# Six jobs instead of five in the lead-in of an attention-plus-FFN kernel, and a new token order for its last two units

## The chip, the cores and the metric

The kernel runs on one core of a Trainium2 chip. The metric is the device time of one execution in microseconds. Three executions of the kernel before took 1590.14, 1590.25 and 1590.91 us; the median is 1590.25 us.

## The reference

`x` has 2048 rows of 512 floats. Two branches read it, and a gate mixes them:

```python
g = sigmoid((x * gate_w).sum(-1, keepdims=True))
# A: 32 query heads of 16, one shared key head and one shared value head
q = (x @ wq).reshape(B, S, 32, 16).transpose(0, 2, 1, 3)
k, v = x @ wk, x @ wv
p = softmax(einsum("bhqd,bkd->bhqk", q, k) * 16 ** -0.5)
a = einsum("bhqk,bkd->bhqd", p, v).transpose(0, 2, 1, 3).reshape(B, S, 512) @ wo
# B: bilinear FFN, 512 -> 1792 -> 512
b = ((x @ w_gate) * (x @ w_up)) @ w_down
out = g * a + (1 - g) * b
```

## The kernel before

**Units.** The attention is cut into 64 units. A unit is one block of 128 query rows for eight heads, which sit in four slots of two. It has 16 steps. For each step two small row-tiled matmuls of the *first pass* (`p1`, L759, then a row maximum on VectorE, L760) and two of the *second pass* (`p2`, L800, then an exponential on ScalarE, L801) are made. One uses the upper half of the array's rows and one the lower half: the kernel calls the halves *lanes* 0 and 1. Matmuls on different lanes run beside each other; matmuls on one lane follow each other. Every two steps, one *token* `p` (`pv`, L813) multiplies the exponentials by V. After a unit's last maximum, four short VectorE instructions (`p1_end`, L765 to L789) and two small DMAs put the row maxima into the unit's query tile, and only then can its second pass begin.

**Jobs.** Everything else that TensorE does is cut into *jobs*: query projections (12 products), FFN gate and up projections (12), down projections (9 or 12) and output projections (12). Each product is done in two halves of 64 rows, one on each lane, into one PSUM bank: first all products of the job on one lane, later all on the other. When both lanes are through, the bank is copied out (`finish`, `evac`). `ffn_jobs` (L606) yields the jobs in a fixed order, so the number of lane slots in the whole program is given; it is only chosen where they stand.

**Front (L826 to L878).** Transposes, the key and value projections and the first two query projections run on the whole array. Between them stand three bursts of maxima, made by `steps(banks)` with 4, 6 and 4 matmuls on the banks that it is given. Together these are 7 of the 16 steps of unit 0.

**Lead-in (the loop at L1063).** Before any second-pass matmul, the first pass must be ahead: `LEAD` is 25 steps per lane. While VectorE works through those maxima, `lead_job` (L1028) and `lead_fill` (L1038, its matmul is L1052) fill TensorE with jobs. At most `OPEN` = 2 jobs may be begun and not ended, and `FIRST` = 5 jobs are begun altogether. A job's second lane may start only when the program can be sure that the first has ended (`E.known`). The last job begun gets one lane only; its other lane is left to the units, so that lane 1 runs one job behind lane 0 from there on. The loop ends when the 25 steps, the five jobs and all second lanes but the last are done. Two transposes of V (`v_late`, L313) also fall into it.

**Units (L1081).** From then on the program follows strings of tokens, one string per unit. `a` and `b` issue a maximum on lane 0 and 1, `c` and `d` a second-pass matmul, `e` and `f` a job's product (L962), `p` the P by V product. Each of the 62 strings `ORDER`, `ORDER_NINE` and `ORDER_AFTER` has 16 each of a, b, c and d, 36 each of e and f, and 8 p. `ORDER_LAST` covers the last two units: 7 a, 7 b, 32 c, 32 d, 72 e, 84 f and 16 p. The tail (L1097) ends the last output projection.

**Queues.** Each engine works its instructions off in the order in which the program emits them: a TensorE instruction that waits for a bank holds back everything behind it. `claim` (L467) picks the bank by a model of when banks come free; on the chip the wait is for the instruction that last read the bank.

Of the kernel before, what the change touches and what calls it, by code (L numbers as in the profile page):

```python
# [31 lines left out]
LEAD = 25  # L32
# [11 lines left out]
PV_IN, PV_ROUND, PV_LAST, PV_END, PV_OUT = 325.0, 866.0, 438.0, 617.0, 647.0  # L44
NB = 8
LAT, LAT_LAST = 1.0, 0.5
FIRST = 5
OPEN = 2


ORDER = (
# [9 lines left out]
    "fcffeeffecffafefcebcfebcfafefdefafccfebfeadeffebcbapppdcbadcppbcbadapppb"  # L61
)
ORDER_LAST = (
    "cdebefebefefedededebbcfefefebefedaefefefadcfefafcfefafefedadefebefedefcf"
    "efcfafabefefedcffefcfefedccfeffcfedefcpppppdedcfefcfcfefefefedefeedcfefe"
    "dfedcpppefedededeffefefededefedefefedcfcffcfefededdefefcfcffedfcfefefefe"
    "fcfpppfcfcffcdfdfcfcdfffccfcfppppp"
)
HALVES = (slice(0, 64), slice(64, 128))
COLS = (slice(0, 256), slice(256, 512))  # L70
# [5 lines left out]
def mix_kernel(ctx: ExitStack, tc: tile.TileContext, x, wq, wk, wv, wo, wg, wu, wd, gw, out):  # L76
# [78 lines left out]
    def mm_all(p, prods, start=True, stop=True):  # L155
        for i, (l, r) in enumerate(prods):
            nc.tensor.matmul(p, l, r, start=start and i == 0, stop=stop and i == len(prods) - 1)  # L157
# [6 lines left out]
    def bank(i, name):  # L164
        return psum.tile([128, 512], F32, name=name, tag=f"bank{i}")
# [130 lines left out]
    def kv(c, b):  # L296
        p = ms_bank(b)
        prods = proj((wkvh, wkvl), xT[c])
        if c == 0:
            prods = prods[0::3] + prods[1::3] + prods[2::3]  # L300
        mm_all(p, prods)
        Kc = KK[:, c * 512:(c + 1) * 512]
        kvs[c] = w512("gs", F32, 3)
        nc.scalar.activation(Kc, p, AF.Identity, bias=kneg)
        nc.scalar.copy(kvs[c], p)
        if c < 2:
            nc.vector.scalar_tensor_tensor(Kc, Kc.bitcast(F32), klow, kvs[c], op0=OP.mult, op1=OP.add)
        else:
            scr = w512("hf", F32, 1)
            nc.gpsimd.tensor_scalar(scr, Kc.bitcast(F32), klow, None, op0=OP.mult)  # L310
            nc.gpsimd.tensor_tensor(Kc, scr, kvs[c], op=OP.add)
# [12 lines left out]
    def v_trans(c, b):  # L324
        pv = bank(b, "pv")
        for t in range(4):
            nc.tensor.transpose(pv[:, t * 128:(t + 1) * 128], kvs[c][:, t * 128:(t + 1) * 128], ident)  # L327
        (nc.vector.tensor_copy if c == 0 else nc.scalar.copy)(
            V[:, c * 4:(c + 1) * 4, 0:DH].rearrange("p t (h d) -> p t h d", h=2),
            pv.rearrange("p (t h c) -> p t h c", t=4, h=2)[:, :, :, 50:58])  # L330
# [88 lines left out]
    def peek():  # L419
        if st["next"] is None and st["gen"] is not None:  # L420
            st["next"] = next(st["gen"], None)
            if st["next"] is None:
                st["gen"] = None
        if front and ready(front[0]) and (len(front) > 1 + (st["f"] > 9) and not st["tail"] or not ready(st["next"])):
            return front[0]
        return st["next"] if ready(st["next"]) else None
# [323 lines left out]
    def p1(k, half, b):  # L750
        u, slot, kq = order1[k]
        c, g, t = units[u]
        q = Q[u]
        if u not in mx:
            mx[u] = work.tile([128, 8, 4], F32, name="mx", bufs=2)
            left[u] = 32
        p = bank(b, "s1")
        r = KROWS[half]
        nc.tensor.matmul(p, q[r, slot], KK[r, kq * 512:(kq + 1) * 512], start=True, stop=True)  # L759
        nc.vector.tensor_reduce(mx[u][:, half * 4 + slot, kq:kq + 1], p, axis=AX.X, op=OP.max)  # L760
        left[u] -= 1
        if left[u] == 0:
            p1_end(u)

    def p1_end(u):  # L765
        q = Q[u]
        m = mm[u % 2]
        nc.vector.tensor_reduce(m[:, 0:8], mx.pop(u), axis=AX.X, op=OP.max)
        w = work.tile([128, 3, 32], F32R, name="mt", bufs=2)
        mt = w[:, 0].bitcast(F32)  # L770
        nc.vector.transpose(mt, m)
        nc.vector.tensor_reduce(w[:, 1], mt.rearrange("p (q v) -> p q v", v=1), axis=AX.X, op=OP.max, negate=True)
        with nc.allow_low_precision(reason="the low part of two that are kept"):
            nc.vector.tensor_reduce(w[:, 2], w[:, 0:2].bitcast(F32).rearrange("p v q -> p q v"), axis=AX.X, op=OP.add)
        end = spend("dve", 800.0)
        d = dram.tile([2, 8, 128], F32, name="dm", tag="dm", bufs=2)

        def store():
            for b in range(4):
                nc.sync.dma_start(d[:, :, b * 32:b * 32 + 32].rearrange("v c q -> c v q"),  # L780
                                  w[b * 32:b * 32 + 8, 1:3].bitcast(F32))
            later(3200, fetch)

        def fetch():
            for half in range(2):
                r = half * 64 + 48
                nc.sync.dma_start(q[r:r + 2].bitcast(F32), d[:, half * 4:half * 4 + 4, :])
            mat[u] = clock["T"] + 4000.0
        later(end - clock["T"] + 300.0, store)  # L789
# [63 lines left out]
    done = 0  # L853

    def steps(banks):
        nonlocal done
        for i, b in enumerate(banks):
            p1(done + i // 2, i % 2, b)
        done += len(banks) // 2

    p = ms_bank(0)
    prods = proj(wqs[1], xT[0])
    mm_all(p, prods[:4], True, False)
    steps((3, 7, 1, 6))
    mm_all(p, prods[4:], False, True)
    qs, qh, ql = w512("wdn", F32, 2), w512("oh", F32R, 2), w512("ol", F32R, 2)
    nc.scalar.copy(qs, p)
# [4 lines left out]
    kv(2, 4)  # L872
    sums.append(gate_mul("wn", 4))
    v_trans(1, 2)
    steps((3, 7, 1, 6))
    kv(3, 0)
    for f in sums:
        f()  # L878
# [11 lines left out]
    qat.update({0: 0.0, 1: 5000.0})  # L890
    st["gen"] = ffn_jobs()
    E = State()
    E.n1, E.dve, E.act = [done, done], 100.0, 3000.0
    E.free = [1700.0, 0.0, 0.0, 0.0, 0.0, 0.0, 200.0, 0.0]
    fetched = 2

# [129 lines left out]
    began, cur = [], [None, None]  # L1026

    def lead_job(l):  # L1028
        if cur[l]:
            return cur[l]  # L1030
        for j in began[:FIRST - 1]:
            if j.first != l and j.done[l] == 0 and j.end is not None and j.end <= E.known:
                return j
        if len(began) < FIRST - l and sum(j.done[1 - j.first] < len(j.items) for j in began) < OPEN and peek():
            return took
# [24 lines left out]

    run, pos, hole, late = [], [0, 0], [0], [0]
    took = object()
    while min(E.n1) < LEAD or len(began) < FIRST or any(cur) or any(j.done[1 - j.first] == 0 for j in began[:-1]):  # L1063
        l = 0 if E.nl[0] <= E.nl[1] else 1
        k = E.n1[l]
        some = (k < LEAD and k <= E.n1[1 - l] + (k >= NJ) and (k < NJ or min(E.n1) >= NJ)
                and max(qat.get(order1[k][0], 1e18), kat[order1[k][2]]) <= clock["T"])
        job = lead_job(l)
        if some and (E.dve < E.nl[l] + 1300.0 or not job) and min(E.free) < E.nl[l]:
            token("ab"[l])  # L1070
        elif job:
            events_until(min(E.nl))
            lead_fill(l)
        else:
            E.nl[l] += 30.0
            events_until(min(E.nl))
    st["lead"] = None
    run += [(began[-1], i) for i in range(len(began[-1].items))]
    pos[0] = len(run)
    is_nine = False  # L1080
    while E.npv < NS:  # L1081
# [15 lines left out]
    while events or front or st["gen"] or st["next"]:  # L1097
        run_events()
        if peek():
            j = take()  # L1100
# [28 lines left out]
```

## Time and profile before

| | us |
|---|---|
| median of three executions | 1590.25 |
| the profiled execution | 1590.37 |
| its span, first to last instruction | 1588.6 |
| TensorE busy | 1582.9 |
| VectorE busy | 1363.4 |
| ScalarE busy | 1203.7 |
| GpSimd busy | 733.3 |

The profiled execution took 1.8 us more than its span, which lies before the first and behind the last instruction. In the rows, PE is TensorE's matmuls, PEld its weight loads, DVE VectorE, ACT ScalarE, POOL GpSimd, SP the engine that issues DMAs; an L with a number is a line of the kernel. Matmuls on different lanes overlap, and each is shown with its whole way through the array, so that a busy PE row says little of how many matmuls were issued in a stretch; it is the starts that count.

### The profile page before, as it was taken

How to read it: one execution, taken by the hardware profiler on the slowest of the kernel's cores; microseconds unless marked ns; L12 is line 12 of the kernel's file. 1: busy time of each engine (PE TensorE's matmuls, PEld its weight loads, DVE VectorE, ACT ScalarE, POOL GpSimd, SP SyncE). 2: the span in 40 equal slices, each digit the busy share in tenths (PEclk: the TensorE clock that was granted, in tenths of full speed). 3: DMA queues.
4: the chain of work that ended last, by engine and by line, in shares of the span. 5: the costliest groups of instructions: out<-in, count | busy, mean ns of one | idle time of the engine just before them, and what ended most of it. 6: DMA issues, size and time to landing. Idle time of an engine off the chain costs nothing.

```text
span 1588.6 us, 35467 instructions
## 1 busy us (share of the span) xinstructions
PE 1582.9 (100%) x13144; PEld 1034.0 (65%) x13144; DVE 1363.4 (86%) x2412; ACT 1203.7 (76%) x2384; POOL 733.3 (46%) x871
## 2 busy tenths in 40 slices
PE   9999999999999999999999999999999999999999
PEld 7775666665665666676675666676675666676675
DVE  6998898898898898898898898888898898888982
ACT  5787787787787787787787787777787787787775
POOL 7535737353633624454532725454442615555440
PEclk9999999999999999999999999999999999999999
DMA  6553322122232212121232212122132212212111
GB/s 196 190 174 119 93 62 74 40 71 58 67 103 79 73 56 67 53 76 54 60 103 72 74 55 73 48 70 66 54 117 65 74 55 74 61 57 59 36 31 42
DMA packets 184995, 121.21 MB, mean 76 GB/s; under 512 B 46197, under 2 KB 154613, under 8 KB 184822
## 3 DMA queue, kind: packets, MB, share of 16 engines
q1 hardware_dynamic: 183620, 118.61, 25.0%
q8 instruction: 104, 1.70, 0.4%
q14 instruction: 69, 0.57, 0.1%
q10 hardware_dynamic: 1202, 0.33, 0.1%
HBM read 82.70 MB, written 36.17 MB: 75 GB/s over the span
## 4 chain that ended last, share of the span: by engine, by line
PE 99%; DVE 1%; DMA 0%; issue 0%; DVEq 0%
PE ms L962 33%; PE acc L813 29%; PE s L800 17%; PE s L759 17%; PE ms L157 1%; PE ms L1052 1%; DVE mx L760 0%; PE px L285 0%; DMA P<-in_A_x_dram 0%; DMA kvn<-in_A_wk_dram 0%; PE wo L157 0%; PE pv L327 0%; PE pick L726 0%; DVE y L737 0%; DVEq L1125 0%
## 5 line engine op out<-in xcount | busy, mean ns | idle before, releaser
L760 DVE TENSOR_REDUCE mx<-s 128x1 f32<-128x512 f32 x2048 | 1289.1, 685 | 172.7 <-PE s L759 94.1
L801 ACT ACTIVATE P<-s 128x512 f32<-128x512 f32 x2048 | 1058.5, 626 | 260.6 <-PE s L800 210.8
L800 PE MATMUL s<-Q,KK 50*128 50x512 f32 x2048 | 703.7, 407 | 0.0
L759 PE MATMUL s<-KK,Q 48*128 48x512 f32 x2048 | 698.4, 401 | 0.2
L813 PE MATMUL acc<-P,V 128*32 128x512 f32 x4096 | 480.5, 597 | 0.0
L800 PEld LDWEIGHTS s<-Q,KK 50*128 50x128 f32 x2048 | 355.8, 185 | 118.4 <-ACT P L801 40.8
L759 PEld LDWEIGHTS s<-KK,Q 48*128 48x128 f32 x2048 | 351.3, 185 | 107.0 <-issue 52.0
L962 PE MATMUL ms<-xh,wl 64*128 64x512 f32 x896 | 319.2, 392 | 0.0
L962 PE MATMUL ms<-xh,wh 64*128 64x512 f32 x896 | 314.2, 393 | 0.0
L962 PE MATMUL ms<-xl,wh 64*128 64x512 f32 x896 | 303.9, 391 | 0.0
L813 PEld LDWEIGHTS acc<-P,V 128*32 128x32 f32 x4096 | 116.8, 109 | 254.8 <-issue 222.8
L397 POOL TENSOR_TENSOR y<-y,yt 128x512 f32<-128x512 f32 x58 | 74.8, 1289 | 212.8 <-ACT yt L396 198.3
L962 PEld LDWEIGHTS ms<-xh,wh 64*128 64x128 f32 x896 | 160.2, 185 | 12.7 <-issue 0.8
L583 POOL TENSOR_TENSOR hf<-gs 128x512 f32<-128x512 f32 x56 | 72.3, 1291 | 203.1 <-ACT gs L572 203.1
L962 PEld LDWEIGHTS ms<-xh,wl 64*128 64x128 f32 x896 | 159.0, 186 | 7.4
L680 POOL TENSOR_TENSOR oT<-raw,rb 128x128 f32<-128x128 f32 x63 | 29.1, 461 | 291.7 <-DMA rb<-dr 285.6
L962 PE MATMUL ms<-wdh,hl 64*128 64x512 f32 x448 | 158.4, 393 | 0.0
L962 PEld LDWEIGHTS ms<-xl,wh 64*128 64x128 f32 x896 | 151.1, 186 | 9.5
L962 PE MATMUL ms<-wdl,hh 64*128 64x512 f32 x448 | 155.3, 394 | 0.0
L962 PE MATMUL ms<-wdh,hh 64*128 64x512 f32 x448 | 155.1, 393 | 0.0
L145 POOL TENSOR_TENSOR wl<-wn,wh 128x512 fp32r<-128x512 f32 x116 | 149.5, 1289 | 9.3
L821 ACT COPY osb<-acc 128x512 f32<-128x512 f32 x63 | 37.0, 588 | 91.5 <-PE acc L813 87.7
(181 smaller groups left out, 1369.3 us busy)
## 6 DMA issues: line engine op xcount, KB each, us to landing
do<-osb SPq DMA_DIRECT2D x63, 256.0 KB
wn<-in_B_w_gate_dram SPq DMA_DIRECT2D x56, 256.0 KB
wn<-in_B_w_up_dram SPq DMA_DIRECT2D x56, 256.0 KB
wdn<-in_B_w_down_dram SPq DMA_DIRECT2D x56, 256.0 KB
Q<-dq SPq DMA_DIRECT2D x384, 32.0 KB
raw<-do SPq DMA_DIRECT2D x252, 32.0 KB
dq<-oh SPq DMA_DIRECT2D x16, 256.0 KB
dq<-ol SPq DMA_DIRECT2D x16, 256.0 KB
```

Of the source, the lines that this page charges most:

```text
L145: nc.gpsimd.tensor_tensor(lo, src, hi.bitcast(F32), op=OP.subtract)
L157: nc.tensor.matmul(p, l, r, start=start and i == 0, stop=stop and i == len(prods) - 1)
L397: nc.gpsimd.tensor_tensor(y[c, t], y[c, t], tmp, op=OP.add)
L583: nc.gpsimd.tensor_tensor(hf, gu[0], gu[1], op=OP.mult)
L680: nc.gpsimd.tensor_tensor(dst, raw[:, 0], rb, op=OP.mult)
L759: nc.tensor.matmul(p, q[r, slot], KK[r, kq * 512:(kq + 1) * 512], start=True, stop=True)
L760: nc.vector.tensor_reduce(mx[u][:, half * 4 + slot, kq:kq + 1], p, axis=AX.X, op=OP.max)
L800: nc.tensor.matmul(p, KK[r, j * 128:(j + 1) * 128], q[r].rearrange("p s q -> p (s q)"), start=True, stop=True)
L801: nc.scalar.activation(P[s][:, half], p, AF.Exp, scale=0.25)
L813: nc.tensor.matmul(acc[u][b:b + 32, :], V[:, j + i], src[:, half], start=(j == 0), stop=(j == NJ - 2))
L821: nc.scalar.copy(osb, acc.pop(u))
L962: nc.tensor.matmul(j.p, lhs[HALVES[l]], rhs[HALVES[l]], start=(l == 0 and i == 0), stop=(l == 1 and end))
```

## The change

Three parts. (1) The bursts of maxima in the front are 5, 6 and 5 matmuls long in place of 4, 6 and 4; the added one stands on bank 5 both times; `steps` now counts matmuls and not steps. (2) In the lead-in, six jobs are begun in place of five, and three may be open at a time in place of two; the condition of the loop now lets the last but one job too be left with lane 1 not begun, and whatever is left so goes to the units. (3) `ORDER_LAST` is a new string with 7 a, 7 b, 32 c, 32 d, 60 e, 72 f and 16 p. The blocks of p in it are 2, 6, 3 and 5 long; they were 5, 3, 3 and 5.

```diff
-FIRST = 5
-OPEN = 2
+FIRST = 6
+OPEN = 3
...
 ORDER_LAST = (
-    "cdebefebefefedededebbcfefefebefedaefefefadcfefafcfefafefedadefebefedefcf"
-    "efcfafabefefedcffefcfefedccfeffcfedefcpppppdedcfefcfcfefefefedefeedcfefe"
-    "dfedcpppefedededeffefefededefedefefedcfcffcfefededdefefcfcffedfcfefefefe"
-    "fcfpppfcfcffcdfdfcfcdfffccfcfppppp"
+    "adefefecfbafefedcbebedefeefedafedefcfefededebafefefefcfafedefebcdefebfae"
+    "fcfedefafebefcfefcfcfeffefcdefedcfcdefcfppcdcdcdppppppfcdeffeededefedffe"
+    "fedefedefedcfefddedcfefefefcfedefeffededefcfefcfcfcpppfcdcfffcfcdffcfcfc"
+    "fdfcfppppp"
 )
...
     def steps(banks):
         nonlocal done
-        for i, b in enumerate(banks):
-            p1(done + i // 2, i % 2, b)
-        done += len(banks) // 2
+        for b in banks:
+            p1(done // 2, done % 2, b)
+            done += 1
...
-    steps((3, 7, 1, 6))
+    steps((3, 7, 1, 6, 5))
...
-    steps((3, 7, 1, 6))
+    steps((3, 7, 1, 6, 5))
...
-    E.n1, E.dve, E.act = [done, done], 100.0, 3000.0
+    E.n1, E.dve, E.act = [done // 2, done // 2], 100.0, 3000.0
...
-    while min(E.n1) < LEAD or len(began) < FIRST or any(cur) or any(j.done[1 - j.first] == 0 for j in began[:-1]):
+    while min(E.n1) < LEAD or len(began) < FIRST or any(cur) or any(j.done[1 - j.first] == 0 for j in began[:-2]) or began[-2].first and not began[-2].done[0]:
...
-    run += [(began[-1], i) for i in range(len(began[-1].items))]
+    run += [(j, i) for j in began if j.done[1] == 0 for i in range(len(j.items))]
```

## Rows read from the trace of the kernel before

**Rows 1.** The page: engines with busy us, share and instructions; shares of the chain.

```profile
PE 1582.9 (100%) x13144; PEld 1034.0 (65%) x13144; DVE 1363.4 (86%) x2412; ACT 1203.7 (76%) x2384; POOL 733.3 (46%) x871
...
PE 99%; DVE 1%; DMA 0%; issue 0%; DVEq 0%
```

**Rows 2.** The chain that ended last, 20 to 75 us: start, us, what.

```profile
39.23 1.17 PE pv L327 x8
...
40.89 6.07 DVE mx L760 x10
...
49.74 0.49 PE s L759
```

**Rows 3.** Busy time by stretch: stretch, its length, busy us (instructions) of each engine.

```profile
35.24:56.61 21.37, 21.12 (x153) 16.37 (x153) 20.47 (x37) 13.44 (x34) 18.92 (x16) 1.00 0.33 120
56.61:72.52 15.91, 15.91 (x130) 13.10 (x131) 15.34 (x28) 14.32 (x29) 5.26 (x6) 1.00 0.74 270
...
81.58:96.28 14.70, 14.70 (x128) 13.14 (x132) 14.23 (x25) 14.43 (x29) 4.54 (x7) 1.00 0.75 250
```

**Rows 4.** Line 1052: duration min/median/max in ns, first and last start.

```profile
L1052 PE MATMUL ms<-hh,wh x20: 383/388/396, 44.2 to 55.9; 64*128 64x512 f32 x20
...
L1052 PE MATMUL ms<-xh,wh x16: 386/394/500, 35.2 to 43.5; 64*128 64x512 f32 x16
```

**Rows 5.** Timeline, one lane's products in a row: start, us, engine, line, what.

```profile
54.00 0.39 PE L1052 MATMUL ms<-hh,wh 64*128 64x512 f32 x1
...
54.23 0.39 PE L1052 MATMUL ms<-hh,wl 64*128 64x512 f32 x1
```

**Rows 6.** Busy time by stretch: two stretches of the lead-in.

```profile
47.65:50.08 2.43, 2.19 (x11) 1.08 (x9) 2.41 (x5) 0.80 (x4) 2.43 (x3) 1.00 0.32 111
...
54.70:56.61 1.91, 1.90 (x11) 1.22 (x10) 1.91 (x4) 1.20 (x3) 1.34 (x2) 1.00 0.26 73
```

**Rows 7.** Timeline of VectorE in and behind the lead-in (idle before, and its releaser).

```profile
36.01 10.94 DVE L760 TENSOR_REDUCE mx<-s 128x1 f32<-128x512 f32 x18 [1.35 <-PE s L759]
...
46.98 0.19 DVE L768 TENSOR_REDUCE mm<-mx 128x8 f32<-128x32 f32 x1
...
51.40 20.39 DVE L760 TENSOR_REDUCE mx<-s 128x1 f32<-128x512 f32 x32
```

**Rows 8.** Timeline of the front around the first and second burst, and one later GpSimd row.

```profile
24.88 0.18 PEld L759 LDWEIGHTS s<-KK,Q 48*128 48x128 f32 x1 [0.18 <-DVE wol L150]
25.14 0.67 ACT L289 COPY osb<-px 128x512 f32<-128x512 f32 x1
...
25.30 0.19 PEld L157 LDWEIGHTS ms<-xh,wl 128*128 128x128 f32 x1 [0.25 <-issue]
...
27.88 3.68 DVE L760 TENSOR_REDUCE mx<-s 128x1 f32<-128x512 f32 x6 [0.63 <-PE s L759]
...
33.75 1.29 POOL L311 TENSOR_TENSOR KK<-hf,gs 128x512 fp32r<-128x512 f32 x1
```

**Rows 9.** Busy time by stretch: the last two units and the tail.

```profile
1536.33:1549.61 13.28, 13.28 (x116) 12.47 (x119) 10.64 (x20) 12.12 (x24) 5.07 (x6) 1.00 0.10 32
1549.61:1554.04 4.43, 4.43 (x43) 1.20 (x42) 0.86 (x2) 1.77 (x4) 0.00 (x0) 1.00 0.05 8
1554.04:1558.21 4.17, 4.17 (x39) 3.31 (x42) 0.00 (x0) 3.64 (x8) 0.46 (x1) 1.00 0.05 16
1558.21:1560.92 2.71, 2.71 (x27) 0.68 (x26) 0.00 (x0) 1.85 (x4) 0.00 (x0) 1.00 0.00 0
1560.92:1569.48 8.56, 8.56 (x72) 7.27 (x75) 1.70 (x3) 8.39 (x17) 0.20 (x1) 1.00 0.33 109
...
1572.19:1575.86 3.67, 3.67 (x28) 2.73 (x31) 0.92 (x2) 3.21 (x7) 0.47 (x1) 1.00 0.06 18
...
1580.29:1588.59 8.30, 4.61 (x57) 3.86 (x56) 3.04 (x7) 0.37 (x1) 0.00 (x0) 0.90 0.10 34
```

**Rows 10.** Timeline of ScalarE across the first block of p there.

```profile
1546.86 4.51 ACT L801 ACTIVATE P<-s 128x512 f32<-128x512 f32 x9
```

## The prediction

> **What bounds the kernel now.** I read the page first: TensorE is busy for nearly the whole span and carries 99% of the chain of work that ended last [rows 1]. A busy TensorE says little here, since two lanes overlap, so I next priced a lane. Where one lane runs alone, its products start 0.23 us apart [rows 5]; the time of a stretch is then the slots of the fuller lane times 0.231 us, plus what is lost. For an ordinary unit this closes: up to its first block of p the string has 62 tokens on lane 0, 62 x 0.231 = 14.3 us, and the stretch took 14.70 us [rows 3]. So the 62 ordinary units are bound by lane slots, and their slots don't change. What can change is the two ends, and there I read the chain in order of time, then stretches, then VectorE's timeline.
>
> The lead-in, 35.24 to 56.61 us, is the one place where the chain leaves TensorE: 6.07 us of it run over ten maxima, and TensorE goes on at 49.74 us after maxima again [rows 2]. VectorE has no idle time there: 18 maxima in 10.94 us (0.60 us each, back to back), then the short instructions that close unit 0 from 46.98 us, then maxima again [rows 7]. TensorE is not full: 47.65 to 50.08 us holds 11 matmuls and 54.70 to 56.61 us another 11, where 21 and 16 had room on two lanes [rows 6]. The reader should see that the first of these is a shortage of jobs, not of time: with two jobs open and neither second lane released, the program could emit only maxima, and those waited for VectorE.
>
> By lanes: line 1052 issued 3 x 20 + 3 x 16 = 108 products (one row of each kind stands in [rows 4]); 60 of them are lane 0's (five jobs of 12). With 18 of the 36 maxima, lane 0 has 78 slots, 18.0 us; the late transposes take 1.2 us [rows 2]; 21.4 - 18.0 - 1.2 leaves 2.2 us lost. The first unit's stretch before its first p, 56.61 to 72.52 us, took 15.91 us against 14.70 us in the next unit [rows 3]: 1.2 us more, because VectorE was still behind. So 3.4 us are lost up to 72.52 us; that is all the room there is for a sixth job.
>
> **Part 1, the bursts.** Each added maximum makes an odd burst, one more slot on the whole-array path: 2 x 0.23 us. But the first burst's fifth stands on bank 5, whose last reader is the ScalarE copy of the last transposed block. That copy runs from 25.14 to 25.81 us, while the burst's fourth matmul loads weights at 24.88 us and the projection behind it resumes at 25.30 us [rows 8]. TensorE works in order, so the fifth waits until about 25.86 us and the eight projection products queue behind it: they resume 0.42 us after the last weight load, as now, so at about 26.28 us, 0.98 us later. That holds the added slot of the first burst too. Bounds: 0.23 us if the copy were out of the way, 1.0 us if it isn't; I take 0.98, since the copy's end is a row. The second odd slot adds 0.23, as bank 5 is then free before its turn. VectorE's idle 0.63 us before the second burst [rows 8] hides the fifth maximum. The key block that the lead-in's first maximum now needs (step 8) is done at 35.04 us [rows 8], later by the same 1 us, and the lead-in begins at 36.45 us: no wait, margin 0.4 us. Sum: lead-in 1.2 us later, two maxima fewer in it. For VectorE that is nothing: 2 x 0.60 = 1.2 us saved, 1.2 us lost at the start.
>
> **Part 2, the lead-in.** Lane 0 now has six jobs of 12 and 17 maxima: 89 slots, 20.6 us, plus 1.2 us of transposes. With a third job open, the starved stretch fills; I take 0.5 us lost in place of 2.2 (bounds 0.2 and 1.5: never none, since the pauses around the transposes and the last job's single lane stay, and not above most of today's). That is 22.3 us from 36.45 us: the lead-in ends at 58.75 us, 2.1 us later. VectorE's 34 maxima and the closing of unit 0 end at about 37.2 + 20.4 + 0.9 = 58.5 us, so it is no longer behind, and the first unit should take 14.8 us in place of 15.9 (bounds 14.7 and 15.4). First p at 73.5 us, 1.0 us later than now; bounds +0.2 and +2.2.
>
> The sixth job is a query projection; its second lane, copy and stores fall into the first unit, as the fifth's did. The fifth's copy moves into the lead-in with one more ScalarE cast and two 256 KB stores on SP's queue, ahead of the stores of x that run there; no unit before the 16th reads what these hold. Nothing is left to the units that they didn't have. I cost this at nothing; were ScalarE held by a cast that waits for one of its two buffers, exponentials would start late, up to about 1 us, which is in the bounds.
>
> On banks I weighed a rule of the Trainium skill. What the row shows is that the stretch with two open jobs ran dry while maxima waited for VectorE [rows 6]. The page TensorEngine Tiling (Array Packing), section Gotcha 1: PSUM Pressure, says that row tiling raises the pressure on PSUM, since different row tiles write to different banks. By it a third open job takes a bank from the maxima, and the lead-in would go on losing its 2.2 us: 1.7 us more than I take, 1590.7 us in all. I stay with 0.5 us, because in the starved stretch jobs were missing and not banks.
>
> **Part 3, the last two units.** Lane 1 is the fuller lane. Its slots between blocks of p are 55, 17, 36 and 15, 123 in all, 28.4 us; the four stretches took 13.28 + 4.17 + 8.56 + 3.67 = 29.7 us [rows 9]. The new string has 56, 3, 37 and 15, 111 in all: 12 fewer, 2.8 us. Blocks of five and three p take 4.43 and 2.71 us [rows 9], 0.86 us for a further p, so blocks of 2, 6, 3 and 5 sum to the same 14.3 us, and both strings change between fill and p equally often. What the new string may add is a wait: before its first block stand 26 exponentials, not 24, of 0.50 us [rows 10]. ScalarE ran 1.8 us past that point before (1546.86 + 4.51 against 1549.61); now about 2.3 us, with one copy fewer. Behind two p (1.85 us) six second-pass matmuls come in three slots and want six banks at once. I take 0.4 us of wait there (bounds 0 and 1.2). Sum -2.4 us, bounds -2.8 and -1.6. The dividing chain of the last but one unit starts and ends earlier with it, and the 8.3 us of the tail [rows 9] stay.
>
> **Sum.** +1.0 - 2.4 = -1.4 us. Against the profiled execution, 1590.37 us, that gives 1589.0 us; the median of the runs lies 0.1 us lower, which I ignore.
>
> **Rivals.** *B, the sixth job is free:* the first p comes no later than 72.5 us and the last units give 2.8 us: 1587.6 us. For it: 3.4 us of loss is there. Against it: 89 slots and a start at 36.45 us leave under 0.3 us of loss for lead-in and first unit together. *C, the gain is eaten:* the lead-in still loses 1.5 us and the last units gain 1.6 us: +2.0 - 1.6, 1590.8 us. For it: 1.2 us of banks held late shows in the first unit even now. *D, two jobs stay open:* the new end of the loop allows lane 1 to be two jobs behind. The new last string makes up one, so 12 slots, 2.8 us, would stand alone behind the last p: -1.4 + 2.8, 1591.8 us. In every unit a third job would hold one of the eight banks until both its lanes are through. From 0.03 us of wait in each of 62 units (1.9 us) this is slower than before by over 0.2%; at 0.1 us it is 1598 us. For it: the condition is written to allow it. Against: the last string has 12 more f than e, just what one job of lag needs, as before. (It is in the units that the pressure named by the Trainium skill's page above would show.)
>
> **How the numbers follow.** A measurement of this kernel can tell about 0.2%, 3.2 us, from no change: below 1587.1 us is faster, above 1593.4 us slower. Forecast 0.52 (its own range 1588.2 to 1590.0), B 0.18, C 0.16, D 0.14. B's better half, with a steady unit or the tail a little shorter too, reaches past 1587.1: 0.10 for faster. D gives 0.12 for slower; the rest, 0.78, is no change that can be told. The range 1586.9 to 1592.0 us leaves out 0.08 below and 0.12 above.
>
> **What would show it.** The first burst's fifth matmul should start at about 25.9 us, the lead-in at 36.4, and line 1052 should show 132 products (120 would be D). No stretch of the lead-in should run on maxima alone. The first p should stand at 73.5 us (72.5: B; above 74.5: C), an ordinary unit's stretch before its first p should stay at 14.7 us, and from the first to the last p of the last two units, with their fill, 41.6 us should pass in place of 43.96. I am wrong if units lengthen, if ordinary units wait for jobs, or if the front is later by another amount than 1.2 us.

## The result and the profile after

The kernel after the change takes 1595.42 us (median of 7 runs, 1594.76 to 1597.31), the kernel before 1590.67 us (median of 7 runs beside it). The ratio is 1.003, with a 95% interval of 1.0021 to 1.004: 4.75 us slower. The forecast was 1589.0 us, and the range ended at 1592.0 us. The profiled execution took 1595.3 us with a span of 1593.5 us, 4.9 us more than the span of before. The table goes through that span by the starts of P by V products, after against before; its first row is contained in the second, and the rows are rounded.

| stretch | after - before, us | forecast |
|---|---|---|
| of the next row: start of the lead-in | +1.05 | +1.2 |
| up to the first p (unit 0 of the second pass) | +5.1 | +1.0 |
| the next two units | +0.7 | 0 |
| units 3 to 60, in small pieces | +0.4 | 0 |
| the third unit from the end, first to last p | +1.5 | 0 |
| the last two units | -2.7 | -2.4 |
| tail | 0 | 0 |
| sum | +4.9 | -1.4 |

The page of the kernel after, engines and chain; it answers to [rows 1]:

```profile
PE 1584.7 (99%) x13144; PEld 1038.4 (65%) x13144; DVE 1363.0 (86%) x2411; ACT 1205.7 (76%) x2386; POOL 733.0 (46%) x871
...
PE 96%; POOL 1%; DMA 1%; issue 0%; ACT 0%; SPq 0%; DVE 0%; DVEq 0%; POOLq 0%; ACTq 0%
```

TensorE is as busy as before, and the averages hardly move. What moves is the chain: GpSimd, DMA, ScalarE and SP's queue now stand in it, each with a share that is small over the whole span. Before, it was TensorE and VectorE [rows 1].

**The front went as forecast.** The first rows are the weight loads at the end of the first burst and at the projection behind it, which answer to [rows 8]; then two rows of line 1052, which answer to [rows 4]; the last is the lead-in by stretch, as in [rows 3] (stretch, length, busy us and instructions of PE, PEld, DVE, ACT, POOL, granted clock, DMA share, GB/s).

```profile
25.73 0.18 PEld L759 LDWEIGHTS s<-KK,Q 48*128 48x128 f32 x1 [0.81 <-ACT osb L289]
26.16 0.19 PEld L157 LDWEIGHTS ms<-xh,wl 128*128 128x128 f32 x1 [0.24 <-issue]
```

```profile
L1052 PE MATMUL ms<-hh,wh x28: 385/393/494, 39.9 to 58.1; 64*128 64x512 f32 x28
...
L1052 PE MATMUL ms<-xh,wh x16: 386/392/496, 36.3 to 47.8; 64*128 64x512 f32 x16
```

```profile
36.29:58.85 22.56, 22.56 (x177) 19.55 (x178) 21.06 (x38) 13.73 (x34) 19.95 (x16) 1.00 0.29 103
58.85:77.65 18.80, 16.89 (x128) 13.66 (x129) 13.99 (x25) 15.58 (x31) 5.33 (x6) 0.91 0.83 295
```

The fifth matmul waits for the copy of L289, 3 x 28 + 3 x 16 = 132 products are made in the lead-in, and it lasts 22.56 us with TensorE busy throughout. The second stretch is the surprise: from the end of the lead-in to the first p 18.80 us pass, not 14.8, TensorE is idle for 1.9 of them, and the mean granted clock is 0.91, where it was 1.00 before [rows 3].

**Why the first unit is late.** Three rows of ScalarE's timeline, three of SP's (its DMA issues; in brackets the idle time before and its releaser), then the chain in order of time:

```profile
59.03 0.59 ACT L372 COPY gs<-ms 128x512 f32<-128x512 f32 x1 [2.13 <-PE ms L1052]
61.61 0.62 ACT L377 CAST oh<-gs 128x512 fp32r<-128x512 f32 x1 [1.99 <-DMA dq<-oh]
62.13 4.01 ACT L801 ACTIVATE P<-s 128x512 f32<-128x512 f32 x8
```

```profile
54.01 4.12 SPq L232 DMA_DIRECT2D Q<-dq  x6
58.17 0.43 SPq L336 DMA_DIRECT2D xd<-hl  x1
59.11 0.34 SPq L216 DMA_DIRECT2D dq<-oh  x1
```

```profile
59.11 2.40 DMA dq<-oh
...
61.61 0.62 ACT oh L377
62.22 0.51 ACT P L801
...
62.77 0.50 PE s L800
```

The fifth job's copy is done at 59.62 us. Its cast (L377) writes a tile `oh` of which there are two, and it needs the one that the third job's cast wrote at 52.69 us. That one is free only when its store to memory has landed. The store stands in SP's queue behind six fetches of a query tile, which take 4.12 us, and one store of x; it is issued at 59.11 and lands at 61.51 us. So the cast waits 1.99 us, and the first exponential stands behind it in ScalarE's queue: 62.13 us, where it was 57.51 us before. In ScalarE's timeline of before, the fifth job's copy comes behind the first exponentials, and its cast is on GpSimd:

```profile
57.51 2.07 ACT L801 ACTIVATE P<-s 128x512 f32<-128x512 f32 x4 [1.57 <-PE s L800]
...
62.97 0.59 ACT L372 COPY gs<-ms 128x512 f32<-128x512 f32 x1
```

TensorE runs out of free banks in the meantime. By stretch, with the granted clock as the third number from the right, and the row in which TensorE goes on:

```profile
62.77 0.50 PE L800 MATMUL s<-Q,KK 50*128 50x512 f32 x1 [1.91 <-ACT P L801]
```

```profile
60.20:62.77 2.57, 0.67 (x5) 0.19 (x2) 1.06 (x2) 1.16 (x3) 0.46 (x1) 1.00 1.03 381
64.00:67.00 3.00, 3.00 (x17) 2.89 (x16) 2.29 (x5) 2.73 (x6) 0.00 (x0) 0.50 1.03 381
67.00:68.00 1.00, 1.00 (x10) 0.99 (x9) 0.40 (x1) 0.61 (x2) 0.00 (x0) 0.80 1.02 383
68.00:70.00 2.00, 2.00 (x20) 1.79 (x18) 1.79 (x3) 2.00 (x5) 1.23 (x2) 1.00 0.13 47
```

TensorE is idle for 1.91 us. From 64.0 to 67.0 us the granted clock is 0.50, the 1.2 GHz level, and 14 matmuls start in those 3 us; from 68 us it is 1.00 again, and 17 start in 2 us. (The counts in the rows take in matmuls that lie only in part in a stretch.) The Trainium skill's page TensorE: Matmul & The Clock Gate, section Part 1: The HAM clock gate, says that idleness brings the engine back to half its clock and work brings it up again; the trace agrees in both directions. The trace of the run that moves the late unit's sum (below) shows the same fall, 0.50 from 64.0 to 67.0 us. It isn't in every execution: some 3 us at half clock lower the mean granted clock of the whole span by 0.001, and two of the seven runs (1594.96 and 1597.31 us) list 1.000.

**The third unit from the end.** One row of VectorE, three of GpSimd:

```profile
1540.00 0.20 DVE L667 RECIPROCAL rc<-den 128x8 f32<-128x8 f32 x1 [3.30 <-POOL den L659]
```

```profile
1532.64 0.61 POOL L144 CAST oh<-oT 128x512 fp32r<-128x512 f32 x1 [15.11 <-PE ms L962]
...
1538.53 1.28 POOL L145 TENSOR_TENSOR hl<-hf,hh 128x512 fp32r<-128x512 f32 x1
1539.76 0.20 POOL L659 TENSOR_TENSOR den<-dn 128x8 f32<-128x8 f32 x1
```

GpSimd too waits for a buffer, 15.11 us at 1532.64 us, and by the profile for products that still read the tile it writes; six long instructions have piled up behind it, and the short sum `den` comes last. VectorE waits 3.30 us for that sum, and the maxima behind it come late. The reciprocal stood at 1530.45 us before, without a wait:

```profile
1530.45 0.20 DVE L667 RECIPROCAL rc<-den 128x8 f32<-128x8 f32 x1
```

From the first to the last p of that unit pass 10.04 us, where it was 8.55.

**The last two units.** By stretch, from fill to block of p in turn; they answer to [rows 9]:

```profile
1544.00:1557.49 13.49, 13.49 (x117) 11.55 (x121) 10.34 (x19) 12.79 (x26) 3.63 (x5) 1.00 0.14 44
1557.49:1559.34 1.85, 1.85 (x18) 0.41 (x18) 0.86 (x2) 1.85 (x5) 0.00 (x0) 1.00 0.26 76
1559.34:1560.24 0.90, 0.90 (x11) 0.57 (x14) 0.00 (x0) 0.74 (x2) 0.00 (x0) 1.00 0.71 248
1560.24:1565.53 5.29, 5.29 (x50) 1.46 (x50) 0.00 (x0) 2.61 (x6) 0.46 (x1) 1.00 0.06 15
```

The fill of 55 tokens took 13.28 us before, the one of 56 takes 13.49 us, and the one of 3 takes 0.90 us where one of 17 took 4.17 [rows 9]. In all 41.2 us pass, 43.96 before.

### The profile page after: what moved, and what is told of

The parts are those of the page before. It is cut to its first block, busy times and chain, and to the rows that moved or that the text cites. A ratio compares the mean times of both kernels' runs of the same rounds, so it can differ in the third digit from the quotient of the medians.

```text
span 1593.5 us, 35462 instructions
## 1 busy us (share of the span) xinstructions
PE 1584.7 (99%) x13144; PEld 1038.4 (65%) x13144; DVE 1363.0 (86%) x2411; ACT 1205.7 (76%) x2386; POOL 733.0 (46%) x871
## 4 chain that ended last, share of the span: by engine, by line
PE 96%; POOL 1%; DMA 1%; issue 0%; ACT 0%; SPq 0%; DVE 0%; DVEq 0%; POOLq 0%; ACTq 0%
PE ms L962 32%; PE acc L813 29%; PE s L759 17%; PE s L800 17%; PE ms L157 1%; POOL yt L344 1%; SPq L232 0%; PE px L285 0%; DMA P<-in_A_x_dram 0%; DMA kvn<-in_A_wk_dram 0%; PE wo L157 0%; POOL KK L311 0%; DMA dq<-oh 0%; POOL hf L310 0%; ACT KK L304 0%
```

## The experiments

Four readings compete. In the texts quoted below, A is the cast that waits for a store, F the longer bursts in the front, D two jobs left open on lane 1 (the rival of the prediction), and J that the lead-in ran dry for want of jobs; other letters are explained where they stand. Ratios are against the kernel before, run on the same chip, with 95% intervals; differences in us are between medians. Diffs are against the kernel after unless said otherwise.

**A third buffer.** The same edit stands at the four places where `oh` is made.

```diff
-        qh, ql = w512("oh", F32R, 2), w512("ol", F32R, 2)
+        qh, ql = w512("oh", F32R, 3), w512("ol", F32R, 2)
```

> The changed kernel with a third buffer for the high part of a split query block (tile oh), nothing else; the order of the program stays. Theory A (in the lead-in's end ScalarE's cast at line 377 waits until 61.61 us for the store that empties one of two oh buffers, and the exponentials queue behind it): the cast runs at once at about 59.6 us, the first exponential starts at about 59.8 in place of 62.13 us, the first P by V product stands at 73.5 to 74.5 in place of 77.65 us, and the time falls by 3 to 4 us to 1591.4 to 1592.4 us. Rival R (three open jobs leave too few banks, so that the first unit is long whatever ScalarE does): cast early, but the first P by V product stays at 77 us or more and the time at 1595.4 us.

Measured: 1591.68 us against 1590.53, ratio 1.0008 (0.9998 to 1.0017). So 3.6 of the 4.75 us are gone. ScalarE's timeline and two stretches:

```profile
59.55 0.62 ACT L377 CAST oh<-gs 128x512 fp32r<-128x512 f32 x1
60.08 0.59 ACT L801 ACTIVATE P<-s 128x512 f32<-128x512 f32 x1
```

```profile
60.00:62.00 2.00, 2.00 (x17) 1.32 (x14) 1.88 (x4) 2.00 (x5) 0.00 (x0) 1.00 1.03 380
...
64.00:66.00 2.00, 2.00 (x20) 1.62 (x17) 1.72 (x4) 2.00 (x6) 0.39 (x1) 1.00 1.03 381
```

The cast doesn't wait, TensorE isn't idle, the clock stays at 1.00, and the first p stands at 74.34 us, 3.24 us earlier. This takes the first unit's loss apart: the first exponential is 2.05 us earlier (the wait), and from it to the first p 14.26 us pass where it was 15.45. These 1.2 us are put down to the lowered clock: in the 4 us from 64 us 21 matmuls start in the kernel after and 32 here, and 11 at this rate are 1.4 us. The third unit from the end shrinks to 8.92 us. The cast on GpSimd has a buffer now, but the instruction behind it still waits, by the program for `ol`, of which there are still two:

```profile
1529.05 1.29 POOL L145 TENSOR_TENSOR ol<-oT,oh 128x512 fp32r<-128x512 f32 x1 [13.92 <-PE s L800]
```

**The old bursts.**

```diff
-    steps((3, 7, 1, 6, 5))
+    steps((3, 7, 1, 6))
...
-    steps((3, 7, 1, 6, 5))
+    steps((3, 7, 1, 6))
```

> The changed kernel with bursts of 4, 6 and 4 maxima as before; lead-in of six jobs, three open, and the new last string stay. Theory A: the front gives its 1.06 us back (lead-in begins at 35.2 in place of 36.3 us), two more maxima in the lead-in cost VectorE 1.2 us; the wait of the cast stays, since the stores stand in the same queue behind the same fetches: first P by V product at 76.5 to 77.7 us, time 1594.3 to 1595.5 us. Rival F (the five-long bursts themselves are what costs): 4 us or more come back, 1591 us.

Measured: 1591.44 us against 1590.53, ratio 1.0005 (0.9996 to 1.0015). By time alone F wins: A had expected 1594.3 to 1595.5 us. The trace shows why both are involved. The lead-in begins 1.07 us earlier (35.22), the store of the third job is issued at 57.63 and not at 59.11 us, and the cast still waits, but for less:

```profile
58.54 0.59 ACT L372 COPY gs<-ms 128x512 f32<-128x512 f32 x1 [2.25 <-PE ms L1052]
59.83 0.62 ACT L377 CAST oh<-gs 128x512 fp32r<-128x512 f32 x1 [0.70 <-DMA dq<-oh]
```

```profile
57.63 0.35 SPq L216 DMA_DIRECT2D dq<-oh  x1
```

TensorE is idle for 0.6 us, and from 60 to 68 us the granted clock stays at 1.00. The first p stands at 74.60 us. A had the mechanism but took the wait as fixed. The bursts set how long it lasts.

**The sum of the third unit from the end on VectorE**, which only moves one short instruction:

```diff
-            nc.gpsimd.tensor_tensor(den, dn[:, 0], dn[:, 1], op=OP.add)
+            (nc.vector if units.index((c, g, t)) == 60 else nc.gpsimd).tensor_tensor(den, dn[:, 0], dn[:, 1], op=OP.add)
```

> The changed kernel with one instruction moved: the 128x8 addition of the denominators of unit 60 (line 659) on VectorE in place of GpSimd. Theory A (at 1536.8 to 1540.0 us VectorE's reciprocal waits 3.3 us for that addition, which stands in GpSimd's queue behind the splits of a job that now come one job earlier; maxima queue behind the reciprocal and TensorE behind them): the stretch from unit 61's first P by V product to the last string shrinks by 1.5 us, first P by V product stays at 77.6 us, time 1593.9 us. Rival P (the 1.5 us are lost because the maxima of the new last string start late for another reason): no change, 1595.4 us.

Measured: 1593.67 us against 1590.53, ratio 1.0018 (1.0009 to 1.0028), 1.6 us of the 4.75 back. The interval meets that of the kernel after (1.0021 to 1.004), so it is the trace that shows the gain: from the first to the last p of that unit pass 8.55 us. Sum and reciprocal:

```profile
1532.58 0.16 DVE L659 TENSOR_TENSOR den<-dn 128x8 f32<-128x8 f32 x1
...
1537.18 0.19 DVE L667 RECIPROCAL rc<-den 128x8 f32<-128x8 f32 x1
```

**A third buffer in the kernel before**, as a control (the diff of the first experiment, against the kernel before):

```diff
-        qh, ql = w512("oh", F32R, 2), w512("ol", F32R, 2)
+        qh, ql = w512("oh", F32R, 3), w512("ol", F32R, 2)
```

> The kernel before with the third oh buffer, nothing else: a control. Before, no cast in the lead-in waits for a store, so theory A and rival R both expect no change, 1590.7 us, first P by V product at 72.5 us. A gain would mean that the buffer pays elsewhere in the run, and that what it brings to the changed kernel isn't the lead-in alone.

Measured: 1591.02 us against 1590.53, ratio 1.0002 (0.9993 to 1.0012), first p at 72.62 us. The buffer brings no gain where the fifth copy comes in the first unit; the change is what made it matter. In this trace the first unit takes 24.21 us from first p to next first p, where it was 23.76, though nothing in its order was changed: a few tenths of a microsecond in one unit of one trace show little.

**Third buffer and old bursts.**

```diff
-    steps((3, 7, 1, 6, 5))
+    steps((3, 7, 1, 6))
...
-        qh, ql = w512("oh", F32R, 2), w512("ol", F32R, 2)
+        qh, ql = w512("oh", F32R, 3), w512("ol", F32R, 2)
```

> Third oh buffer and bursts of 4, 6 and 4: what the longer bursts are worth when no cast waits, against the run with the third buffer alone (first P by V product 74.34 us, 1591.7 us). Theory S (the fifth maximum's wait for bank 5 costs the front 1.06 us, and two maxima fewer save VectorE 1.2 us, so that they are worth nothing): first P by V product 73.6 to 74.6 us, time 1590.8 to 1591.8 us. Rival G (the bursts do pay where the cast doesn't hide it): first P by V product at 75.3 us or later, time 1592.7 us.

Measured: 1589.98 us against 1590.57, ratio 0.9997 (0.9988 to 1.0007); better than expected. Each against the kernel before beside it, its median is 1.7 us better than with the third buffer alone, though the two intervals overlap. Only 0.5 us of that is the first p (73.82 us); 0.9 us stands between the second and third unit, which take 23.75 us instead of 24.62.

**Third buffer, and the first burst's fifth maximum on bank 4**, so that it doesn't wait for the copy of L289:

```diff
-    steps((3, 7, 1, 6, 5))
+    steps((3, 7, 1, 6, 4))
```

> Third oh buffer, and the first burst's fifth maximum on bank 4 in place of bank 5; bank 4's last copy ends at about 24.8 us, 1 us before bank 5's. Theory S: the lead-in begins at 35.5 in place of 36.24 us, and the first P by V product comes 0.4 to 0.8 us earlier, 73.6 to 73.9 us; time 1591.0 us. Rival K (the front's extra 1.06 us is the price of an odd burst on the whole array, whatever the bank): lead-in at 36.2 us, first P by V product at 74.3 us, time 1591.7 us.

Measured: 1590.77 us against 1590.57, ratio 1.0003 (0.9994 to 1.0013). The burst is no longer interrupted:

```profile
24.30 1.20 PE L759 MATMUL s<-KK,Q 48*128 48x512 f32 x5
25.43 0.50 PE L157 MATMUL ms<-xh,wl 128*128 128x512 f32 x1
```

The projection goes on at 25.43 us, the lead-in starts at 35.56, and the first p stands at 73.65 us. That is the best first p with the longer bursts, but the units behind it take 24.52 us in one place, as in the first experiment.

**The fifth job's cast on GpSimd**, with the two buffers as they are:

```diff
-            if st["lead"] is None:
+            if st["lead"] is None or st["q"] == 4:
```

> The changed kernel with two buffers as it was; only the fifth query projection that ends in the lead-in is split on GpSimd, as it was in the kernel before, and not by a cast on ScalarE. Theory A (it is this one cast, in ScalarE's queue ahead of the exponentials, that holds the first unit): the first exponential starts at 59.6 to 60.1 in place of 62.13 us, first P by V product 73.8 to 74.5 us, time 1591.0 to 1592.0 us; the stretch of unit 61 stays long (10.0 us from first to last P by V product). Rival W (the store that lands at 61.5 us holds something else too, the query tile of a later unit or SP's queue): less than 1.5 us comes back, time above 1594 us.

Measured: 1591.62 us against 1590.57, ratio 1.0006 (0.9996 to 1.0015). This separates the wait from its place in a queue:

```profile
59.11 0.59 ACT L372 COPY gs<-ms 128x512 f32<-128x512 f32 x1 [2.12 <-PE ms L1052]
59.59 4.53 ACT L801 ACTIVATE P<-s 128x512 f32<-128x512 f32 x9
```

```profile
61.93 0.61 POOL L144 CAST oh<-gs 128x512 fp32r<-128x512 f32 x1 [3.53 <-DMA dq<-oh]
```

```profile
59.00:63.00 4.00, 4.00 (x34) 2.96 (x32) 3.05 (x6) 3.89 (x9) 0.99 (x2) 1.00 0.94 343
```

GpSimd is idle for 3.53 us ahead of the cast. The copy ends at 59.70 us, so 2.2 us of that are a wait for the same store, no shorter than ScalarE's was. It holds up no exponential, since none stands behind it. TensorE isn't idle, the clock stays at 1.00, and the first p stands at 74.13 us. With the buffer or with the other queue, the same 3.6 to 3.7 us come back.

**Cast on GpSimd, old bursts and the sum on VectorE.**

```diff
-            if st["lead"] is None:
+            if st["lead"] is None or st["q"] == 4:
...
-    steps((3, 7, 1, 6, 5))
+    steps((3, 7, 1, 6))
...
-            nc.gpsimd.tensor_tensor(den, dn[:, 0], dn[:, 1], op=OP.add)
+            (nc.vector if units.index((c, g, t)) == 60 else nc.gpsimd).tensor_tensor(den, dn[:, 0], dn[:, 1], op=OP.add)
```

> Three at once, as a version to beat both: the fifth query projection split on GpSimd, bursts of 4, 6 and 4, and unit 60's denominators added on VectorE. Theory A with S and the reading of unit 61: the gains of the runs before add up, 1595.4 - 4.1 - 0.3 - 1.7 = 1589.3 us, 1.2 us under the kernel before. Rival: they overlap (the old bursts and the cast heal the same wait), and the first unit stays 2 us late: 1590.5 to 1591 us, no better than before.

Measured: 1590.13 us against 1590.57, ratio 0.9996 (0.9987 to 1.0005). The first p stands at 73.19 us and the late unit takes 8.56 us, but the second unit takes 24.55 us again, and the time is 0.8 us above the expected 1589.3.

**All of these, and the gate's short instructions a little earlier.** The step that ends the gate (one ScalarE and three VectorE instructions, L360 to L363) is placed by the program's clock; where it falls among the maxima shifts with the front.

```diff
-        qh, ql = w512("oh", F32R, 2), w512("ol", F32R, 2)
+        qh, ql = w512("oh", F32R, 3), w512("ol", F32R, 2)
...
-            if st["lead"] is None:
+            if st["lead"] is None or st["q"] == 4:
...
-            nc.gpsimd.tensor_tensor(den, dn[:, 0], dn[:, 1], op=OP.add)
+            (nc.vector if units.index((c, g, t)) == 60 else nc.gpsimd).tensor_tensor(den, dn[:, 0], dn[:, 1], op=OP.add)
...
-    steps((3, 7, 1, 6, 5))
+    steps((3, 7, 1, 6))
...
-    later(70000.0, gates)
+    later(69000.0, gates)
```

> A version to beat both: lead-in of six jobs, three open, and the new last string; bursts of 4, 6 and 4; third oh buffer; the lead-in's fifth split on GpSimd; unit 60's denominators added on VectorE; the gate's three VectorE instructions asked for 1 us earlier in the program's own clock, because in the runs with the sixth job VectorE waits 0.58 us for ScalarE there and that unit takes 24.5 us in place of 23.75. Theory A with all readings so far: first P by V product 73.1 us, unit 1 to unit 2 23.8 us, time 1589.2 to 1589.6 us, 1.0 to 1.4 us under the kernel before. Rival: the gate isn't what makes that unit long; time 1590.1 us as in the run without the shift.

Measured: 1589.58 us against 1590.61, ratio 0.9992 (0.9983 to 1.0001). The second unit takes 23.96 us. The first p stands at 73.40 us, 0.3 us later than expected, and the first unit takes 24.73 us: a query tile is not there in time, and TensorE waits for its transfer.

```profile
83.50 0.58 PE L800 MATMUL s<-Q,KK 50*128 50x512 f32 x2 [0.51 <-DMA Q<-dm]
```

An earlier front is not the reason, since the run before this one has its first p earlier still and takes 23.89 us there. What differs in the traces is SP's queue: a store of x ahead of that transfer held it for 2.42 us, and for 0.56 us in the run before. The profiled execution took 1590.24 us, one of the longest of eleven, so this loss need not be in each.

**Two open jobs, as before.** Cast on GpSimd and old bursts, with `OPEN` back at 2. It asks whether the third open job is what fills the lead-in.

```diff
-OPEN = 3
+OPEN = 2
...
-            if st["lead"] is None:
+            if st["lead"] is None or st["q"] == 4:
...
-    steps((3, 7, 1, 6, 5))
+    steps((3, 7, 1, 6))
```

> Six jobs in the lead-in but only two open at a time, with bursts of 4, 6 and 4 and the fifth split on GpSimd; against the run with three open (first P by V product 73.2 us, line 1052 from 34.9 to 57.7 us). Theory J (in the lead-in of before jobs were missing, because two were open and neither second lane was released): a stretch of maxima alone comes back, and the lead-in ends 1.5 to 2.5 us later, at 59.2 to 60.2 us, with the first P by V product at 74.7 to 75.7 us. Rival B (banks are what is scarce, so that a third open job gains nothing): lead-in's end within 0.5 us of 57.7 us.

Measured: 1827.46 us against 1590.61, ratio 1.1493 (1.1477 to 1.1508). Line 1052, a stretch of the lead-in that answers to [rows 6], and three waits (engine and line, what it waited for, us in total, times, longest):

```profile
L1052 PE MATMUL ms<-hh,wh x24: 383/392/396, 44.0 to 59.0; 64*128 64x512 f32 x24
```

```profile
47.72:49.94 2.22, 1.96 (x8) 0.85 (x6) 2.22 (x5) 0.58 (x2) 2.22 (x3) 1.00 0.34 121
```

```profile
PEld s L800 <- ACT P L801: 84.6, 229, 0.9
...
PEld s L759 <- ACT P L801: 69.0, 170, 0.9
PEld s L759 <- DVE mx L760: 51.1, 76, 0.8
```

On the lead-in J is right: with two open jobs the dry stretch is back (6 matmuls start in its 2.22 us, 8 in the 2.43 us of before), and the lead-in ends at 59.7 us, though it began at 35.1. The first p stands at 76.2 us, later than J had it. The rest is a surprise, as the loop then ends with two jobs open on lane 1 (3 x 24 + 3 x 16 = 120 products, the sign that the prediction gave for D). So this run is rival D, made real. From the third unit to the third from the end a unit takes 27.3 us, not 23.8, 3.4 us more in each. The three waits above are all for a bank that ScalarE or VectorE has not yet read; in the kernel before they are 40.8, 24.3 and 1.7 us in all. They grow by 138 us here. That fits a lack of banks, though no run separates the banks from the lag of the jobs. Over the whole kernel, 210 of the 237 us are lost between the first p and that of the third unit from the end, 21 in the tail. The rule that the prediction drew from the Trainium skill's page TensorEngine Tiling (Array Packing), section Gotcha 1: PSUM Pressure, agrees with this, in the units. In the lead-in of the kernel after it does not: with three open jobs TensorE was busy throughout.

**Third buffer, old bursts, sum on VectorE**, with the gate where it was:

```diff
-        qh, ql = w512("oh", F32R, 2), w512("ol", F32R, 2)
+        qh, ql = w512("oh", F32R, 3), w512("ol", F32R, 2)
...
-    steps((3, 7, 1, 6, 5))
+    steps((3, 7, 1, 6))
...
-            nc.gpsimd.tensor_tensor(den, dn[:, 0], dn[:, 1], op=OP.add)
+            (nc.vector if units.index((c, g, t)) == 60 else nc.gpsimd).tensor_tensor(den, dn[:, 0], dn[:, 1], op=OP.add)
```

> Third oh buffer, bursts of 4, 6 and 4, unit 60's denominators added on VectorE; ScalarE's cast in the lead-in stays, as does the gate's place. Against the run without the moved addition (1590.0 us; 8.9 us from first to last P by V product of unit 61). Theory A with the reading of unit 61: that stretch falls to 8.55 us and the time by 0.35 us, to 1589.6 us, 1.0 us under the kernel before. Rival: the addition only mattered where GpSimd waited for the second oh buffer; no change, 1590.0 us.

Measured: 1589.62 us against 1590.71, ratio 0.9995 (0.9986 to 1.0003). The first p stands at 73.77 us, the second unit takes 23.73 us, the late one 8.55 us. No unit is late any more, and the difference of the medians is -1.1 us. The prediction had -1.4 us for the whole change, with the longer bursts, which this kernel lacks; and the interval still holds 1.

**Third buffer, and the gate much earlier.**

```diff
-    later(70000.0, gates)
+    later(65500.0, gates)
...
-        qh, ql = w512("oh", F32R, 2), w512("ol", F32R, 2)
+        qh, ql = w512("oh", F32R, 3), w512("ol", F32R, 2)
```

> The third oh buffer alone, as in the first run, and the gate's instructions asked for 4.5 us earlier, where VectorE has gaps between two blocks of P by V products. Theory Q (unit 1 to unit 2 takes 24.6 us in place of 23.75 because VectorE waits 0.58 us for the gate's exponential and then works 0.9 us on the gate while TensorE's maxima queue): that unit takes 23.8 us, and the time falls by 0.8 us, from 1591.7 to 1590.9 us. Rival: the loss has another cause and stays, at 24.6 us and 1591.7 us.

Measured: 1591.26 us against 1590.71, ratio 1.0004 (0.9995 to 1.0013). VectorE's row of the gate, first in the kernel after and with the third buffer alone, then here:

```profile
111.69 0.17 DVE L361 TENSOR_SCALAR gb<-gb 128x16 f32<-128x16 f32 x1 [0.57 <-ACT gb L360]
...
108.16 0.17 DVE L361 TENSOR_SCALAR gb<-gb 128x16 f32<-128x16 f32 x1 [0.58 <-ACT gb L360]
```

```profile
103.04 0.17 DVE L361 TENSOR_SCALAR gb<-gb 128x16 f32<-128x16 f32 x1 [1.34 <-ACT gb L360]
```

The second unit takes 23.94 us instead of 24.62, though VectorE waits longer at the new place (1.34 us): there it costs little. So some 0.7 us hang on where these instructions fall. The other traces bear it out: the six with the wait of 0.57 or 0.58 us, the kernel after's among them, have 24.35 to 24.62 us in this unit, and six with no wait there, the kernel before's among them, 23.74 to 24.05 us. The times of this run and of the third buffer alone are not told apart.

## Why the prediction was wrong

**Part 1, right on the front.** The fifth maximum waited for the copy, the projection went on at 26.16 us and the lead-in began 1.05 us later (forecast 1.2). Without the wait, on bank 4, the lead-in begins 0.7 us earlier, as the bounds had it. With the old bursts it also begins 1.1 us earlier, but ends only 0.5 us earlier (58.1 against 58.6 us at the last product). What the prediction did not follow is where the later lead-in puts a store in SP's queue: against the kernel before, the old bursts alone bring back 3.8 us (+0.9 in place of +4.75), since the wait that is told next shrinks to 0.70 us.

**Part 2, the lead-in itself, right.** It ended at 58.85 us; the forecast was 58.75. By the prediction's own slots it lost 0.8 us (22.56 - 20.6 - 1.2), where 0.5 was taken and 2.2 was lost before. The run with two open jobs shows the same dry stretch as the kernel before, so the reading of [rows 6] as a shortage of jobs holds. The 11 matmuls read there count some that began before the stretch; 8 start in it (9 in the second), so it was drier still.

**Part 2, what the sixth job moves: the step that failed.** The prediction said of the fifth job's copy, cast and stores: "I cost this at nothing; were ScalarE held by a cast that waits for one of its two buffers, exponentials would start late, up to about 1 us, which is in the bounds." The mechanism was named and its size was wrong. The wait was 1.99 us and not 1. The prediction names no row for its end; the store that frees the buffer had 4.12 us of fetches ahead of it in SP's queue. And the wait wasn't the end of the cost. TensorE was idle 1.91 us and its clock went to 0.50 for over 3 us, 1.2 us more. Together with the wait that is 3.24 us, which the third buffer brings back; a wait of 0.70 us (old bursts) brought no fall of the clock. Removing the wait by a buffer, or taking it out of ScalarE's queue, gives the same first p within 0.2 us (74.34 and 74.13 us).

**Part 2, the first unit, wrong.** The prediction took 14.8 us for the first unit up to its first p in place of 15.9, as VectorE would have caught up. Without any wait of the cast (third buffer, with either bursts), 15.8 us pass from the last product of the lead-in to the first p, as in the kernel before (56.6 to 72.4 us). So the first p stood at 74.3 us in place of the forecast 73.5. Why the unit isn't shorter is not settled. VectorE, with 20 maxima in 13.8 us (59.88 to 73.68 us, third buffer alone), was not working back to back at 0.60 us each. Copy and cast hold ScalarE for 1.1 us ahead of the first exponential even without a wait, at 60.08 us; but where the cast is on GpSimd the first exponential starts 0.5 us earlier and the first p only 0.2 us.

**The ordinary units, wrong.** "62 ordinary units are bound by lane slots, and their slots don't change" is right as to the slots. But where the work of other engines falls changed with the front. The late unit's sum came behind a cast that waited for an `oh` buffer: 1.5 us, shown by moving it (8.55 us, as before). With the third buffer, the gate's instructions cost 0.7 us, shown by moving them. In the kernel after, the first two units lose 0.7 us as well, 0.4 and 0.3. The wait for the gate stands in the second of them, but the gate was not moved alone there, and the control lost 0.45 us in its first unit without the change. So this share, and another 0.4 us in small pieces, stay open.

**Part 3, right.** 41.2 us from the first to the last p with their fill, forecast 41.6; the wait of 0.4 us that was set behind the two p didn't come (0.90 us for three slots, 0.69 by their price).

**The rivals.** B did not come: no kernel with the sixth job had its first p before 73.19 us. C's mechanism, jobs still missing or banks held in the lead-in, was not seen: the lead-in lost 0.8 us, where C had 1.5. D did not occur in the changed kernel (132 products, not 120). Its price was far too low: 3.4 us in each unit where it was made to occur, against the 0.03 to 0.1 us that the prediction weighed.

The profiled span lies 6.3 us above the forecast (+4.9 against -1.4). Of these, about 3.2 are the cast's wait with its clock, 0.9 the first unit, 1.5 the late sum, 0.7 and 0.4 the other units; the last two units gave 0.3 more than forecast. The kernels that keep the sixth job and the new last string and take the two named waits away stand at -1.0 to -1.1 us against the kernel before, which can't be told from no change. They also leave out the longer bursts; with these the best is +0.2 us (bank 4). So no run shows the sum of -1.4 us, not even with the waits gone.

## What to carry to other kernels

A step that is moved earlier brings its buffers along: for each tile that it writes, find the last reader, and if that is a DMA, count what stands ahead of it in the issuing queue. A wait costs what stands behind it in its queue, so the cheapest mend can be another engine that has nothing urgent, and not a shorter wait. And a kernel bound by slots is only steady while the other engines' work stays where it was: after a shift, look at the units one by one, for the same slots can take a microsecond more.

## What the runs showed of the hardware

An idle stretch of 1.91 us on TensorE, in a kernel that had been busy until then, was followed by 3 us at a granted clock of 0.50, beginning some 1.2 us after work had gone on. Two traces show it, and two of seven executions were without it; in the run with 0.6 us of idle time there was none. Six issues of small fetches held SP's queue for 4.12 us, and a 256 KB store behind them took 2.40 us from its issue to landing. In the run that leaves one job more unfinished, and with it one bank more held, a unit took 27.3 us in place of 23.8, 14% more, and its waits for banks grew by 138 us in all.
